# The first product of layer 2 by seven products of halves, weights streamed from DRAM

## The chip, the cores and the metric

The kernel runs on one core of a Trainium2 chip. Its time is the device time of one execution, in microseconds. The engines of the core have short names here: PE is TensorE's matmul (PEld its weight load), DVE VectorE, ACT ScalarE, POOL GpSimd, SP SyncE, which issues the DMAs.

## What is computed

Pooled attention, and behind it two feed-forward layers without residuals. All arrays are fp32; there are 4 batches, 8 heads, 576 positions of 64, hence 2304 tokens of 512, and both layers widen to 2048.

```python
def _attn_ref(q, k, v):
    k_p = k.reshape(B, H, Sp, pool, D).mean(axis=3)
    v_p = v.reshape(B, H, Sp, pool, D).mean(axis=3)
    scores = scale * np.matmul(q, k_p.transpose(0, 1, 3, 2))
    scores = scores - np.max(scores, axis=-1, keepdims=True)
    attn = np.exp(scores)
    attn = attn / (np.sum(attn, axis=-1, keepdims=True) + 1e-09)
    return np.matmul(attn, v_p)

def _moe_ref(x, w_in, w_out):          # layer 1
    h = x @ w_in
    g = np.where(h >= 1, h, np.where(h <= -1, 0.0, (h + 1) ** 2 / 4.0))
    return g @ w_out

def _moe2_ref(x, w_in, w_out):         # layer 2
    h = x @ w_in
    g = np.maximum(h, 0.0) + np.log1p(np.exp(-np.abs(h)))
    return g @ w_out
```

## The kernel before

The tokens are cut into five blocks of 512, 512, 512, 384 and 384 (BLK), the 2048 inner columns into 16 chunks of 128. Layer 1 runs block by block, chunk by chunk; layer 2 does the same after it. A chunk is one first product (emit_g1, matmul L387: four slices of the 512 inputs, out `h` in a PSUM bank), an activation (act) and one second product (emit_g2, matmul L452, summed over the 16 chunks in the PSUM banks `y`). The second product lags two chunks behind the first, so that PE has work while the activation runs.

But for the first block of layer 1, an fp32 operand is split into a high and a low part (whi and wlo of a weight, xh and xl of an input, gh and gl of an activation), and a product is three matmuls: high by high, high by low, low by high. In layer 2 the first product of a chunk is 12 matmuls of the block's 512 or 384 columns; the second takes 128 tokens at a time, three matmuls of 512 columns each. The activation of layer 2 (L411 to L432) is Abs, Exp and Ln on ACT, a subtraction on POOL (r), four operations on DVE and the split into gh and gl, on ACT and DVE.

Weights come as 64-bit floats. Those of layer 2 are converted during layer 1 in 32 units (convert2, L158; two words on ACT, exponents on DVE, a product on POOL, a sum and a split) that start at half step CONV2 = 48, three in ten half steps, and are stored to DRAM (`w2d`). In the last block of layer 1 w2_load (L182) brings them back, and they stay in SBUF during layer 2 as 32 tiles of the pool `w`. The output of layer 1 is split as it leaves PSUM (emit_y, L459: four ACT and four DVE operations a block), stored to `y1d`, and read back by x2_load (L364).

PE and SP follow the order of the code throughout. In layer 1 so do ACT, DVE and POOL (`order`), with the attention of the next block, the conversion units and the loads laid between the chunks by the tables PLAN, KV_PLAN and CONV2; in layer 2 a scheduler orders ACT, DVE and POOL.

Of the kernel before, what the change touches and what calls it, by code (L numbers as in the profile page):

```python
# [20 lines left out]
NP = H // 2  # L21
# [9 lines left out]
def pooled_attention_ffn_ffn(ctx, tc, q, k, v, v0, w1, w2, out):  # L31
# [26 lines left out]
    CONV2 = 48  # L58
    T0 = [sum(BLK[:j]) for j in range(NB)]
    TB = 128 * max(BLK)  # L60
# [11 lines left out]

    y1d = dram.tile([128, NB, 2, KD, TB], FP32, name="y1d")
    w2d = dram.tile([128, NC, 2, 2, DM], FP32, name="w2d")
# [17 lines left out]
    later = []  # L92

# [33 lines left out]
    def convert1(m):  # L127
# [10 lines left out]
        wt[0, *USE[m]] = af.rearrange("p (h f) -> p h f", h=2)  # L138
        yield

    def split1(m):

        hi, lo = (slot([128, 2, DM], FP32R, n) for n in ("whi", "wlo"))
        f = wt[0, *USE[m]]
# [3 lines left out]
        wt[0, *USE[m]] = (hi, lo)  # L148
        yield
# [7 lines left out]

    def convert2(n):  # L158
        a = es2.cv.tile([128, DM], U32, tag="a", bufs=3, name="a")
# [12 lines left out]
        b = es2.cv.tile([128, DM], U32, tag="b", name="b")  # L172
        hi, lo = b.bitcast(FP32R), a.bitcast(FP32R)
        nc.scalar.activation(out=hi, in_=af, func=ACTF.Copy)
        yield
        nc.vector.tensor_tensor(out=lo, in0=af, in1=hi.bitcast(FP32), op=ALU.subtract)
        yield
        for m, t in enumerate((hi, lo)):
            nc.sync.dma_start(out=w2d[:, n // 2, m, n % 2, :], in_=t.bitcast(FP32))
        yield  # L180

    def w2_load(m):  # L182
        wt[1, *USE[m]] = tuple(slot([128, 2, DM], FP32R, n) for n in ("whi", "wlo"))
        for n, t in enumerate(wt[1, *USE[m]]):
            nc.sync.dma_start(out=t.bitcast(FP32), in_=w2d[:, m, n])
# [63 lines left out]
    def kv_gen(b):  # L249
# [3 lines left out]
        if b > 1:  # L253
            for job in jobs[:3] if ring else jobs:
                kv_load(b, *job, ring)
            yield
        for m, job in enumerate(jobs):
# [3 lines left out]
            if ring and 0 < m < len(jobs) - 2:  # L261
# [10 lines left out]
    def tile_gen(i, j, wide=False):  # L272
# [85 lines left out]
    def x_tiles(f, j):  # L358
        xs[f, j] = (
# [4 lines left out]
    def x2_load(j):  # L364
        n = 128 * BLK[j]
        x_tiles(1, j)
        for m, x in enumerate(xs[1, j]):
            nc.sync.dma_start(out=x.bitcast(FP32)[:, :, 0:n], in_=y1d[:, j, m, :, 0:n])

    def whole(f, j):  # L370

        return (f, j) == (0, 0)

    def emit_g1(f, j, c):
        n = 128 * BLK[j]
        h = ps["h" if f == 0 or c % 2 else "h2"].tile([128, TB], FP32, tag="h", name="h")[:, 0:n]
        done = 0
        for kk in range(KD):
            cols = slice(kk * 128, (kk + 1) * 128)
            if whole(f, j):  # L380
                ops = ((wt[f, 0, c // 2][:, c % 2, cols], xs[f, j][0].bitcast(FP32)),)
            else:
                wh, wl = (t[:, c % 2, cols] for t in wt[f, 0, c // 2])
                xh, xl = xs[f, j]
# [319 lines left out]
```

## Time and profile before

| | us |
|---|---|
| three runs | 918.67, 918.76, 920.44 |
| median | 918.76 |
| the profiled execution | 918.5 |
| its span | 916.8 |
| PE / DVE / ACT / POOL busy | 892.3 / 541.1 / 486.6 / 137.1 |

The span is the time from the first to the last instruction of the profiled execution; the device time has 1.7 us around it. Busy times are sums over the whole span, while the kernel has stages with different limits (attention, layer 1 with the conversion beside it, layer 2), so the stretches of 20 us below tell more than the sums. In the timeline a matmul's duration overlaps the next one's, since matmuls are pipelined: what one costs is the distance of starts. A wait in the profile names the line that waits and the operation whose end released it.

### The profile page before, as it was taken

How to read it: one execution, taken by the hardware profiler on the slowest of the kernel's cores; microseconds unless marked ns; L12 is line 12 of the kernel's file. 1: busy time of each engine (PE TensorE's matmuls, PEld its weight loads, DVE VectorE, ACT ScalarE, POOL GpSimd, SP SyncE). 2: the span in 40 equal slices, each digit the busy share in tenths (PEclk: the TensorE clock that was granted, in tenths of full speed). 3: DMA queues.
4: the chain of work that ended last, by engine and by line, in shares of the span. 5: the costliest groups of instructions: out<-in, count | busy, mean ns of one | idle time of the engine just before them, and what ended most of it. 6: DMA issues, size and time to landing. Idle time of an engine off the chain costs nothing.

```text
span 916.8 us, 12048 instructions
## 1 busy us (share of the span) xinstructions
PE 892.3 (97%) x4442; PEld 715.2 (78%) x4442; DVE 541.1 (59%) x887; ACT 486.6 (53%) x931; POOL 137.1 (15%) x121
## 2 busy tenths in 40 slices
PE   8999999999999999899899899999999999999998
PEld 4444445788878888899899788888888888999896
DVE  6898773758678555767656434454445444544544
ACT  4766544566655545566655444444444443554544
POOL 0000000001111111111111112222222222222221
PEclk9999999999999999999999899999999999999999
DMA  7844510302465235424799910030003000300000
GB/s 255 331 149 163 207 44 37 125 12 69 143 224 185 85 111 195 146 97 140 258 397 395 341 54 0 1 138 1 1 0 115 1 1 1 116 0 1 35 1 35
DMA packets 37547, 105.64 MB, mean 115 GB/s; under 512 B 3888, under 2 KB 7984, under 8 KB 34672
## 3 DMA queue, kind: packets, MB, share of 16 engines
q1 hardware_dynamic: 37488, 104.87, 32.3%
q8 instruction: 35, 0.57, 0.3%
q14 instruction: 24, 0.20, 0.1%
HBM read 73.92 MB, written 30.93 MB: 114 GB/s over the span
## 4 chain that ended last, share of the span: by engine, by line
PE 83%; DVE 7%; ACT 4%; DMA 4%; issue 1%; POOL 0%; SPq 0%; DVEq 0%; ACTq 0%; POOLq 0%
PE y L452 39%; PE h L387 38%; DMA w2d<-b 2%; PE a L338 2%; PE a L324 2%; PE a L280 2%; DMA st<-in_w 2%; ACT e L313 1%; DVE gl L432 1%; DVE y L467 1%; DVE wf L108 1%; DMA kv<-in_k 1%; DVE ks L217 1%; PE vpa L243 1%; DVE wf L137 0%
## 5 line engine op out<-in xcount | busy, mean ns | idle before, releaser
L387 PE MATMUL h<-xh,whi 128*128 128x512 f32 (+1 forms) x576 | 213.4, 370 | 0.0
L387 PE MATMUL h<-xh,wlo 128*128 128x512 f32 (+1 forms) x576 | 210.7, 366 | 0.0
L387 PE MATMUL h<-xl,whi 128*128 128x512 f32 (+1 forms) x576 | 210.4, 365 | 0.0
L420 POOL TENSOR_TENSOR r<-e,r 128x512 f32<-128x512 f32 (+1 forms) x80 | 95.5, 1194 | 314.9 <-DVE r L417 296.9
L430 ACT ACTIVATE gh<-l 128x512 fp32r<-128x512 f32 (+1 forms) x80 | 47.1, 589 | 141.4 <-DVE l L425 137.8
L387 PEld LDWEIGHTS h<-xh,whi 128*128 128x128 f32 x576 | 108.3, 188 | 15.5 <-issue 1.6
L387 PEld LDWEIGHTS h<-xl,whi 128*128 128x128 f32 x576 | 108.3, 188 | 14.1 <-issue 0.5
L387 PEld LDWEIGHTS h<-xh,wlo 128*128 128x128 f32 x576 | 108.1, 188 | 12.7
L452 PE MATMUL y<-whi,gl 128*128 128x512 f32 x288 | 113.9, 395 | 1.5 <-DVE gl L432 1.5
L452 PE MATMUL y<-whi,gh 128*128 128x512 f32 x288 | 112.9, 392 | 2.0 <-ACT gh L430 2.0
L452 PE MATMUL y<-wlo,gh 128*128 128x512 f32 x288 | 113.5, 394 | 0.0
L165 POOL TENSOR_TENSOR l<-l,st 128x512 bf16<-128x512 bf16 x32 | 40.1, 1254 | 456.5 <-DVE st L112 390.6
L452 PE MATMUL y<-gl,whi 128*128 128x512 f32 (+1 forms) x256 | 93.9, 367 | 9.3 <-DVE gl L432 9.2
L398 ACT ACTIVATE t<-h 128x512 f32<-128x512 f32 (+1 forms) x80 | 44.5, 556 | 100.4 <-PE h L387 94.7
L452 PE MATMUL y<-gh,whi 128*128 128x512 f32 (+1 forms) x256 | 94.9, 371 | 0.0
L452 PE MATMUL y<-gh,wlo 128*128 128x512 f32 (+1 forms) x256 | 93.0, 363 | 0.0
L417 DVE TENSOR_SCALAR r<-e 128x512 f32<-128x512 f32 (+1 forms) x80 | 32.9, 412 | 95.0 <-ACT e L415 95.0
L432 DVE TENSOR_TENSOR gl<-l,gh 128x512 fp32r<-128x512 f32 (+1 forms) x80 | 52.1, 652 | 55.2 <-ACT gh L430 54.5
L414 ACT ACTIVATE e<-h 128x512 f32<-128x512 f32 (+1 forms) x80 | 44.5, 556 | 65.8 <-PE h L387 61.2
L404 DVE SCALAR_TENSOR_TENSOR t<-t,h 128x512 f32<-128x512 f32 (+1 forms) x64 | 39.5, 617 | 60.8 <-ACT t L399 60.6
L425 DVE TENSOR_TENSOR l<-l,r 128x512 f32<-128x512 f32 (+1 forms) x80 | 51.0, 638 | 36.7 <-POOL r L420 36.3
L452 PEld LDWEIGHTS y<-whi,gl 128*128 128x128 f32 x288 | 54.6, 189 | 13.8 <-DVE gl L432 2.4
(76 smaller groups left out, 1324.9 us busy)
## 6 DMA issues: line engine op xcount, KB each, us to landing
raw<-in_w SPq DMA_DIRECT2D x16, 1024.0 KB, 4.8
st<-in_w SPq DMA_DIRECT2D x32, 512.0 KB, 4.4
w2d<-b SPq DMA_DIRECT2D x32, 256.0 KB, 4.7
w2d<-a SPq DMA_DIRECT2D x32, 256.0 KB, 4.9
whi<-w2d SPq DMA_DIRECT2D x16, 512.0 KB, 8.6
wlo<-w2d SPq DMA_DIRECT2D x16, 512.0 KB, 8.8
y1d<-y SPq DMA_DIRECT2D x12, 512.0 KB, 3.8
kv<-in_k SPq DMA_DIRECT2D x16, 288.0 KB, 5.3
```

Source lines behind the costliest of these rows:

```text
L165: nc.gpsimd.tensor_tensor(out=l, in0=l, in1=e, op=ALU.mult)
L280: nc.tensor.matmul(out=pa[off:off + n, r * 512 + p * T:r * 512 + (p + 1) * T], lhsT=qt[rows, p, off:off + n], rhs=kps[b][rows, p, :], star ...
L387: nc.tensor.matmul(out=h, lhsT=a, rhs=b[:, kk, 0:n], start=(done == 0), stop=(done == len(ops) * KD - 1),)
L398: nc.scalar.activation(out=g, in_=h, func=ACTF.Relu, bias=1.0)
L404: nc.vector.scalar_tensor_tensor(out=g, in0=t, scalar=1.0, in1=h, op0=ALU.min, op1=ALU.max)
L414: nc.scalar.activation(out=e, in_=h, func=ACTF.Abs)
L417: nc.vector.tensor_scalar(out=r, in0=e, scalar1=1.0, scalar2=-1.0, op0=ALU.add, op1=ALU.add)
L420: nc.gpsimd.tensor_tensor(out=r, in0=e, in1=r, op=ALU.subtract)
L425: nc.vector.tensor_tensor(out=g, in0=g, in1=r, op=ALU.add)
L430: nc.scalar.activation(out=gh, in_=g, func=ACTF.Copy)
L432: nc.vector.tensor_tensor(out=gl, in0=g, in1=gh.bitcast(FP32), op=ALU.subtract)
L452: nc.tensor.matmul(out=o, lhsT=a, rhs=b, start=(c == 0 and n == 0), stop=(c == NC - 1 and n == len(ops) - 1),)
```

## The change

Layer 2 no longer goes by blocks. The tokens form three groups of 768 (NS), each two halves of 384 (SN), and the chunks are taken in pairs, eight pairs, so layer 2 has 24 steps (NQ). In a step the first product is a product of 2 x 2 blocks: token halves by halves of the 512 inputs, by halves of the pair's columns. It is computed with seven products (PRODUCTS, emit_product) in place of eight, by the scheme of Strassen and Winograd: x_gen builds the sums and differences of the input's blocks (four DVE operations, and seven splits on ACT and DVE) from the unsplit y1, convert2 those of the weights (t1 to t4). The seven products go to two PSUM banks in turn; ACT keeps three intermediate results (`s`) and copies the last, DVE adds three times (L828), and act2 does the activation on the two chunks, 128 x 768 each.

The second product (emit_group, six tiles of 128 tokens a half step) is laid between the seven products as filler: two tiles after each of the first five products, one after the last two; in a step the tiles of (step before last, half 1) come first, then those of (last step, half 0).

The weights no longer stay in SBUF: a step loads its own (wi_load, four DMAs, and wo_load, two, 2.88 MB together), two steps ahead for wi, so each weight is read three times. DRAM holds seven split blocks of weights for each pair (`wid`). x_gen for the first group runs in the last block of layer 1; for the others from the third step of the group before. emit_y now copies (two ACT, two DVE operations a block). CONV2 is 44. `ob` has the pool's two buffers instead of four, and `kv` and `q` of the attention have fewer buffers as well.

```diff
-    CONV2 = 48
+    CONV2 = 44
+    NS, SN = 3, 384
...
+            t = slot([128, 4, QK], FP32, "t")
+            t3, t2, t4, t1 = (t[:, m, :] for m in range(4))
+            nc.vector.tensor_tensor(out=t1, in0=b12, in1=b11, op=ALU.subtract)
+            nc.vector.tensor_tensor(out=t3, in0=b22, in1=b12, op=ALU.subtract)
+            yield
+            nc.vector.tensor_tensor(out=t2, in0=b22, in1=t1, op=ALU.subtract)
+            nc.vector.tensor_tensor(out=t4, in0=b21, in1=t2, op=ALU.subtract)
...
+    def wi_load(q, i):
+        n = min(2, NPR - 2 * i)
+        t = slot([128, n, 2, QK], FP32R, "wi")
+        nc.sync.dma_start(out=t.bitcast(FP32), in_=wid[:, q % NH, 2 * i:2 * i + n])
...
+        def hi(p, f):
+            if s == 1 and p < 4:
+                t = xpool.tile([128, 2, 2, SN], FP32R, tag=("xh", "xl")[p % 2], name="xf")
+                x2[s, p] = (t[:, 0], t[:, 1])
+            else:
+                x2[s, p] = tuple(slot([128, 2, SN], FP32R, n) for n in ("xfh", "xfl"))
+            nc.scalar.activation(out=x2[s, p][0], in_=f, func=ACTF.Copy)
+
+        def lo(p, f):
+            h, l = x2[s, p]
+            nc.vector.tensor_tensor(out=l, in0=f, in1=h.bitcast(FP32), op=ALU.subtract)
...
+        a22, a21 = load(1, 1), load(1, 0)
+        yield
+        a11, a12 = load(0, 0), load(0, 1)
+        yield
+        hi(3, a22)
+        yield
+        lo(3, a22)
+        s1 = a22
+        tt(s1, a21, a22, ALU.add)
...
+    for o in (8, 9, *range(12, 23)):
+        plan.setdefault(32 * LAST + o, []).append(("x", 0))
...
+    PRODUCTS = (0, 1, 0, 1, 0, 1, 0)
+    FRESH = (0, 1, 5)
+    def emit_product(q, p, o):
+        wh, wl = (wi[q, p][:, m, :] for m in range(2))
+        xh, xl = x2[q // NH, p]
+        done = 0
+        for kk in range(2):
+            cols = slice(kk * 128, (kk + 1) * 128)
+            for a, b in ((wh, xh), (wh, xl), (wl, xh)):
+                nc.tensor.matmul(
+                    out=o, lhsT=a[:, cols], rhs=b[:, kk, :],
+                    start=(p in FRESH and done == 0), stop=(done == 5),
...
-                ob = es2.t2.tile([128, DM], FP32, tag="ob", bufs=4, name="ob")
+            ob = es2.t2.tile([128, DM], FP32, tag="ob", name="ob")
...
+        for p, o in enumerate(banks[b] for b in PRODUCTS):
+            emit_product(q, p, o)
+            if p < 3:
+                keep[p] = gpool.tile([128, SN], FP32, tag=("t", "gh", "gl")[p], name="s")
+                nc.scalar.activation(out=keep[p], in_=o, func=ACTF.Copy)
+            elif p < 6:
+                h, x = ((ha[:, SN:], 2), (hb[:, SN:], 1), (ha[:, 0:SN], 0))[p - 3]
+                nc.vector.tensor_tensor(out=h, in0=o, in1=keep[x], op=ALU.add)
+            else:
+                nc.scalar.activation(out=hb[:, 0:SN], in_=o, func=ACTF.Copy)
+            if p == 5:
+                act2(q, 0, ha)
+            if p == 6:
+                act2(q, 1, hb)
+            if q == NQ - 1:
+                filler(1)
+            else:
+                filler(2 if p < 5 else 1)
...
+            if p == 2:
+                wo_load(q)
+            if q + 2 < NQ and p % 2 + (p == 6):
+                wi_load(q + 2, p // 2)
+            if xg and p in (1, 3, 5):
+                next(xg, None)
```

Three places show how instructions stand now. The first is ACT at the start of layer 2. Before, Abs (L414), Exp (L415) and Ln (L416) of the first two chunks stand between the four copies of layer 1's output (L466):

```order
L414 ACTIVATE e<-h 128x512 x2
L466 ACTIVATE y<-y_3726 128x384
L415 ACTIVATE e<-e 128x512
L466 ACTIVATE y<-y_3727 128x384
L415 ACTIVATE e<-e 128x512
L466 ACTIVATE y<-y_3728 128x384
L416 ACTIVATE l<-e 128x512
L466 ACTIVATE y<-y_3729 128x384
L416 ACTIVATE l<-e 128x512
```

On ACT in the changed kernel the same place, the first step (h_4508 is half 0, h_4509 half 1 of its result; L825 keeps an intermediate result, L830 copies the last product):

```order
L825 ACTIVATE s<-h 128x384 x3
L557 ACTIVATE y<-y_3859 128x384
L557 ACTIVATE y<-y_3861 128x384
L593 ACTIVATE e<-h_4508 128x768
L830 ACTIVATE h_4509<-h 128x384
L594 ACTIVATE e<-e 128x768
L593 ACTIVATE e<-h_4509 128x768
L825 ACTIVATE s<-h 128x384
L595 ACTIVATE l<-e 128x768
L594 ACTIVATE e<-e 128x768
L595 ACTIVATE l<-e 128x768
L602 ACTIVATE gh<-l 128x768 x2
```

Abs and Exp of half 1 and a copy of the next step now stand ahead of the Ln of half 0, and both gh come last.

The second place is PE in the first step of layer 2. Before, the first of the second product's matmuls (L452) follow twelve matmuls of a chunk's first product:

```order
L387 MATMUL h<-xh,whi 128x512
L387 MATMUL h<-xl,whi 128x512
L387 MATMUL h<-xh,wlo 128x512
L452 MATMUL y_4486<-whi,gh 128x512
L452 MATMUL y_4486<-wlo,gh 128x512
L452 MATMUL y_4486<-whi,gl 128x512
L452 MATMUL y_4487<-whi,gh 128x512
```

On PE in the changed kernel, the last matmuls of layer 1 (L543), and the first products (L582) that follow them without filler:

```order
L543 MATMUL y_3862<-gh,whi 128x384
L543 MATMUL y_3862<-gl,whi 128x384
L543 MATMUL y_3862<-gh,wlo 128x384
L582 MATMUL h<-xfh,wi 128x384
L582 MATMUL h<-xfl,wi 128x384
L582 MATMUL h<-xfh,wi 128x384 x2
L582 MATMUL h<-xfl,wi 128x384
L582 MATMUL h<-xfh,wi 128x384 x2
```

Twenty-four matmuls of L582 stand there in a row (the last three products of the first step, which have no filler, and the first product of the second), until the first tile of the second product comes, which needs gh of half 0:

```order
L582 MATMUL h<-xfl,wi 128x384
L582 MATMUL h<-xfh,wi 128x384
L619 MATMUL y_4645<-whi,gh 128x512
L619 MATMUL y_4645<-wlo,gh 128x512
L619 MATMUL y_4645<-whi,gl 128x512
L619 MATMUL y_4646<-whi,gh 128x512
L619 MATMUL y_4646<-wlo,gh 128x512
L619 MATMUL y_4646<-whi,gl 128x512
```

From there on six matmuls of 384 and mostly six of 512 alternate.

The third place is DVE in the last block of layer 1. Before, a chunk's two operations (L404, L432) stand beside one unit of the conversion:

```order
L404 SCALAR_TENSOR_TENSOR t<-t,h 128x384
L432 TENSOR_TENSOR gl<-t,gh 128x384
L170 TENSOR_TENSOR a<-a,l 128x512
L107 TENSOR_SCALAR st<-a 128x512
L108 SCALAR_TENSOR_TENSOR a<-a,st 128x512
L112 TENSOR_SCALAR st<-a 128x512
L404 SCALAR_TENSOR_TENSOR t<-t,h 128x384
L432 TENSOR_TENSOR gl<-t,gh 128x384
```

On DVE in the changed kernel (L264 and L267 are x_gen's, L220 the splits of weights, L118 to L184 a conversion unit):

```order
L517 SCALAR_TENSOR_TENSOR t<-t,h 128x384
L527 TENSOR_TENSOR gl<-t,gh 128x384
L220 TENSOR_TENSOR t<-t,b 128x512
L118 TENSOR_SCALAR st<-a 128x512
L119 SCALAR_TENSOR_TENSOR a<-a,st 128x512
L123 TENSOR_SCALAR st<-a 128x512
L264 TENSOR_TENSOR xfl<-x_3957,xfh 128x768
L220 TENSOR_TENSOR t<-t,b 128x512
L220 TENSOR_TENSOR a<-a,b 128x512
L264 TENSOR_TENSOR xfl<-x_3981,xfh 128x768
L267 TENSOR_TENSOR x_3955<-x_3955,x_3981 128x768
L517 SCALAR_TENSOR_TENSOR t<-t,h 128x384
```

Nine operations, three of a conversion unit, three splits of weights and three of x_gen, now stand between two chunks' activations there; before it was four.

## Rows read from the trace of the kernel before

**Rows 1.** The page: busy time, share of span and instructions of each engine

```profile
PE 892.3 (97%) x4442; PEld 715.2 (78%) x4442; DVE 541.1 (59%) x887; ACT 486.6 (53%) x931; POOL 137.1 (15%) x121
```

**Rows 2.** The page: the chain that ended last, shares by engine

```profile
PE 83%; DVE 7%; ACT 4%; DMA 4%; issue 1%; POOL 0%; SPq 0%; DVEq 0%; ACTq 0%; POOLq 0%
```

**Rows 3.** Stretches of 20 us: PE, PEld, DVE, ACT, POOL busy, clock, DMA share, GB/s

```profile
440.00:460.00 20.00, 17.26 (x100) 16.94 (x99) 14.95 (x27) 11.53 (x23) 3.81 (x3) 1.00 0.82 273
460.00:480.00 20.00, 18.15 (x105) 17.83 (x104) 10.60 (x19) 10.26 (x20) 2.65 (x2) 1.00 1.03 408
480.00:500.00 20.00, 19.49 (x112) 19.09 (x111) 15.02 (x25) 11.53 (x23) 3.82 (x3) 1.00 1.02 391
...
520.00:540.00 20.00, 17.14 (x64) 13.54 (x65) 9.99 (x16) 7.49 (x13) 4.17 (x3) 0.83 0.50 188
540.00:560.00 20.00, 20.00 (x90) 16.57 (x89) 9.03 (x15) 9.50 (x16) 3.88 (x3) 1.00 0.01 1
```

**Rows 4.** PE's waits, 505 to 917 us: total, times, longest

```profile
PE y L452 <- ACT gh L430: 2.0, 1, 2.0
PE y L452 <- DVE gl L432: 1.5, 1, 1.5
```

**Rows 5.** Timeline of PE, start of layer 2: start, duration, instruction

```profile
508.86 0.39 PE L387 MATMUL h<-xh,whi 128*128 128x512 f32 x1
...
511.62 0.39 PE L387 MATMUL h<-xh,whi 128*128 128x512 f32 x1
...
514.34 0.33 PE L452 MATMUL y<-gh,whi 128*128 128x384 f32 x1
...
518.98 0.39 PE L387 MATMUL h<-xh,wlo 128*128 128x512 f32 x1
...
528.58 0.40 PE L387 MATMUL h<-xl,whi 128*128 128x512 f32 x1
```

**Rows 6.** Timeline of all engines, the last instructions

```profile
912.51 0.40 PE L452 MATMUL y<-whi,gl 128*128 128x512 f32 x1
912.94 0.60 ACT L475 ACTIVATE ob<-y 128x512 f32<-128x512 f32 x1 [0.79 <-PE y L452]
```

**Rows 7.** Timeline of PE in the blocks of 384 tokens of layer 2

```profile
835.19 0.39 PE L452 MATMUL y<-whi,gh 128*128 128x512 f32 x1
...
837.27 0.33 PE L387 MATMUL h<-xh,whi 128*128 128x384 f32 x1
...
838.34 0.33 PE L387 MATMUL h<-xh,whi 128*128 128x384 f32 x1
...
839.38 0.39 PE L452 MATMUL y<-whi,gh 128*128 128x512 f32 x1
...
843.50 0.33 PE L387 MATMUL h<-xh,whi 128*128 128x384 f32 x1
```

**Rows 8.** Groups by line and form: busy us, mean ns, idle before; 1024 wide: 0-140 us

```profile
L415 ACT ACTIVATE e<-e 128x512 f32<-128x512 f32 x43 | 27.2, 632 | 1.3
L414 ACT ACTIVATE e<-h 128x384 f32<-128x384 f32 x31 | 15.3, 492 | 15.9 <-PE h L387 15.7
L145 ACT ACTIVATE whi<-wf 128x1024 fp32r<-128x1024 f32 x16 | 16.7, 1045 | 0.0
L421 DVE SCALAR_TENSOR_TENSOR l<-h,l 128x512 f32<-128x512 f32 x43 | 29.7, 691 | 9.8 <-ACT l L416 9.8
L421 DVE SCALAR_TENSOR_TENSOR l<-h,l 128x384 f32<-128x384 f32 x31 | 17.3, 558 | 5.7 <-ACT l L416 5.7
L108 DVE SCALAR_TENSOR_TENSOR wf<-wf,b 128x1024 uint32<-128x1024 uint32 x16 | 19.6, 1225 | 0.6
L420 POOL TENSOR_TENSOR r<-e,r 128x512 f32<-128x512 f32 x48 | 63.1, 1315 | 212.0 <-DVE r L417 194.0 <-PE y L452 18.0
```

**Rows 9.** DMA issues: times, KB each, median us to landing

```profile
out<-ob SPq DMA_DIRECT2D x18, 256.0 KB, 2.1
```

**Rows 10.** PE's waits, 140 to 509 us: total, times, longest

```profile
PE y L452 <- DVE gl L432: 9.2, 6, 2.7
```

More of the change, by code (lines that the diff above doesn't have):

```diff
@@ L92, in pooled_attention_ffn_ffn @@
     later = []
+    wi = {}
+    wo = {}
+    x2 = {}
     def slot(shape, dtype, name):
@@ L188, in batch_runs @@
+        yield
+        hi(6, s4)
+        yield
+        lo(6, s4)
+        yield
     def batch_runs(i):
@@ L362, in x_tiles, with whole, emit_g1 @@
         )
-    def x2_load(j):
+    def whole(j):
+        return j == 0
+    def emit_g1(j, c):
         n = 128 * BLK[j]
[L366 to L376, printed above, removed]
+        h = ps["h"].tile([128, TB], FP32, tag="h", name="h")[:, 0:n]
         done = 0
@@ L663, in pooled_attention_ffn_ffn @@
-    while pend:
-        emit_g2(*pend.pop(0))
+        if hot and c + 2 < NC:
+            next(c1[c + 2])
+        step(n - 1)
+        for g in splits:
+            next(g)
+        splits = []
+        step(n - 2)
+        if hot and c + 1 < NC:
+            next(c1[c + 1])
+        if hs == CONV2 - 4:
+            st_load(0)
+            st_load(1)
+        if hs >= CONV2:
+            tick(hs % 10 in (0, 3, 6))
+        background(hs)
+        while len(pend) > 2:
+            emit_g2(*pend.pop(0))
@@ new lines, in pooled_attention_ffn_ffn @@
+        step(n - 1)
+        next(acts[n])
+        if hot and c + 1 < NC:
+            next(c1[c + 1])
+        if hot and c + 4 < NC:
+            w_load(c + 4)
+        if hs + 1 >= CONV2:
+            tick((hs + 1) % 10 in (0, 3, 6))
+        background(hs + 1)
+        if j == 0 and c >= NC - 2 or j == 1 and c < NC - 2:
+            splits = [split1((c + 2) % NC)]
+            next(splits[0])
+        if j == LAST and c in (11, 12, 13, 14):
+            for i in range(2):
+                wi_load((c - 11) // 2, (c - 11) % 2 * 2 + i)
@@ new lines, in pooled_attention_ffn_ffn, with filler @@
+    while flight:
+        tick(False)
+    order.close()
+    esc.close()
+    es1.close()
+    es2.t2 = es2.enter_context(tc.tile_pool(name="t2", bufs=2))
+    ps["y2"] = es2.enter_context(tc.tile_pool(name="ps_y2", bufs=1, space=PSUM))
+    for m in (NB * NC - 2, NB * NC - 1):
+        for _ in acts.pop(m, ()):
+            pass
+    fill = [(emit_g2, (*s, (m,))) for s in pend for m in range(KD)]
+    NQ = NS * NH
+    xg = None
+    def filler(n):
+        for _ in range(min(n, len(fill))):
+            f, args = fill.pop(0)
+            f(*args)
@@ L665, in pooled_attention_ffn_ffn @@
+    for o, w in ((1, 1), (0, 0), (0, 1)):
+        fill += [(emit_group, (NQ - 1 - o, w, t)) for t in range(2 * SN // 128)]
+    filler(len(fill))
     es2.close()
```

371 lines of the change are left out of this document (204 added, 167 removed).

## The prediction, made before the changed kernel ran

> **What bounds the kernel now.** The page's busy shares come first: PE is at work for 892.3 of 916.8 us, the next engine, DVE, for 541 [rows 1]. The chain of work that ended last agrees: 83% of it is PE [rows 2]. Such shares are means, so the second view cuts the trace into stretches of 20 us. In layer 2 PE is busy all the time (20.00 of 20.00 at 540), ACT and DVE about half of it and DMA near nothing [rows 3]; the list of PE's waits from 505 us on holds only 2.0 and 1.5 us, both at the start of layer 2 [rows 4]. So layer 2 is priced by its matmuls. The end of layer 1 is different: from 440 to 500 PE loses 2.7, 1.9 and 0.5 us of each 20 while the DMA share is 0.82 to 1.03 and DVE is at 15 of 20 [rows 3].
>
> The profiled execution took 918.5 us for a span of 916.8; the median of the three runs is 918.76. I work in differences and add them to the 918.5, 0.3 under the median and well inside the 0.2% that I count as no change.
>
> **Part 1, the matmuls of layer 2.** First what they cost now. The first of layer 2 starts at 508.86, the last at 912.51 [rows 5, 6], with its own step of 0.23 that is 403.9 us. Not part of them are the 12 narrow matmuls that finish layer 1 (2.1 us) and the stall at the start: between the start at 518.98 and that at 528.58 lie 13 matmuls [rows 5], worth 13 x 0.229 = 3.0 of the 9.6 us, so about 6.4 is lost (waiting, and then matmuls at twice the usual spacing: the granted clock of 520 to 540 is 0.83, part of it at the lower of the two levels [rows 3]). There remain 395.4 us.
>
> The spacing of starts gives the price of one: in a chunk of two blocks that alternate, 12 matmuls of 384 columns take 837.27 to 839.38 = 2.11 us, the first six of them 1.07; 18 of 512 take 839.38 to 843.50 = 4.12, so 0.229 each [rows 7]; in an unbroken run of the wide ones 12 take 511.62 to 514.34 = 2.72, so 0.2267 [rows 5]. The new layer 2 has 24 steps of 7 products. A product is six matmuls of 384, between them stand 36 matmuls of 512 a step. At 1.07 for every six and 0.2315 for a 512 (nine of 512 between two stretches of 384, 835.19 to 837.27, run at that) a step is 7 x 1.07 + 36 x 0.2315 = 15.83 us, 24 steps 380.0. **That is -15.4 us**, although an eighth of the first product, 24 x 6 x 0.176 = 25 us, is gone: most of today's first product runs in 512 columns at 0.2267, which is 4.43 ns for ten columns, and 384 in 0.176 are 4.58; and the unbroken runs of 24 are cut into pieces of six, where each change of shape and back costs about 0.06, 7 times a step. The bounds: if the change of shape cost nothing, a step would be 42 x 0.1733 (the six from 838.34 to 839.38) + 36 x 0.2267 = 15.44, the sum 370.6, -24.8; if it cost twice as much, 390, -5.
>
> The Trainium skill, page "TensorE: Matmul & The Clock Gate", section "Back-to-back issue gap", gives an isolated matmul N/2.4 + 2.5 ns: 162.5 for 384 columns and 215.8 for 512. Worked out from it (an estimate), the saving would be 22.8. The rows show 173 to 178 and 227 to 231, so the trace does not agree, and its spacing decides; that page's time is near the one of rival (b).
>
> **Part 2, the other engines of layer 2.** A step adds three ACT copies and one to SBUF (384 wide, 0.49 each) and three DVE additions (0.56 each), and does the activation on tiles of 768. Durations of 768 lie between the rows of 512 and 1024 [rows 8]: ACT 0.63 and 1.05 give 0.84, DVE 0.69 and 1.23 give 0.96; POOL at 512 takes 1.32, so 1.97. ACT: 4 x 0.49 + 2 x 4 x 0.84 = 8.7 of 15.8 us; DVE: 3 x 0.56 + 2 x (3 x 0.96 + 0.6) = 8.6; POOL 3.9. None is near the bound. Latency matters more. From p5's last matmul to the first gh go a DVE addition, Abs, the copy of p6, Exp, Abs of the other half, a copy, Ln, two DVE operations on the half, the r of the other and gh: 0.43 + 0.56 + 0.84 + 0.49 + 0.84 + 0.84 + 0.49 + 0.84 + 0.96 + 0.6 + 0.96 + 0.84, with hand-overs about 9.2 us. In the steady state PE has five products and eight tiles (8 x 3 matmuls of 512) until it needs that gh: 5 x 1.07 + 24 x 0.2315 = 10.9. So the chain hides, with about 2 us to spare, gl a little less; the two PSUM banks come free 1.6 us or more before their next product. Weights: 2.88 MB a step in 15.8 us are 182 GB/s, under half of the 391 to 408 that the trace reaches [rows 3], and each load is issued 17 us or more of matmuls ahead of its use. I take zero for all of this. If the cover is gone, each step pays the difference, 24 x the shortfall.
>
> **The start of layer 2** has no such cover. Eight quarter chunks of layer 1 fill the first four products; then p4, p5, p6 and the p0 of the next step run bare, and the tiles of (step 0, half 0) wait for the chain above with only 2 x 1.07 + 0.23 us of work beside it: 9.2 - 2.4 = 6.8 us, gl 0.6 more. In the row a wait of 2 us and one of 1.5 drew matmuls at double spacing until 528.58, a loss of about 2.4 on top [rows 5]; I add 2.5. In the second step the additions queue on DVE behind those of x_gen for the next group (0.8), and in the third its half 0 is late again by about 1.5 and gl by 3.2, since x_gen's DVE operations wait for a load there and hold the queue, with 0.5 of clock loss. Sum 15.8, against 6.4 today: **+9.4**, bounds +3 (the later steps pay nothing and the first chain is 2 us shorter) and +13.
>
> **The tail.** Now the last matmul starts at 912.51, its copy ends at 913.54 and the span at 916.8, so 4.3 us [rows 6]. The last group has six tiles instead of three and ob has two buffers instead of four: a copy of the third and fifth tile waits until a store has landed, 2.1 us after its issue [rows 9]. Tile 1: copy to +1.1, landed about +3.5; tile 3: +4.1 and +6.5; tile 5: +7.1 and +9.5; tile 6 +10.5 on the other chain, counted from the start of tile 1's last matmul, while the last matmul starts at +3.45. So 7.3 instead of 4.3: **+3**. Bounds 0 (stores land at once) and +4.
>
> **Layer 1.** Gone: the weights' and inputs' loads in the last block, whose queue kept DMA at 0.89 to 1.03 [rows 3]. I give back 2.4 (what PE loses from 460 to 500) and 1.1 of the 2.7 of 440 to 460: -3.5. The bursts at a block's end are halved (no split of y1), -2 of the 9.2 us that PE waits there for gl [rows 10], a guess between 0 and -4. Added: for each of the eight pairs of chunks four DVE additions of 256 columns (some 0.42) and 1.1 us more of splits, 2.8 us, 22.6 in all, spread over blocks 1 to 4; and x_gen for group 0 in the last block, 11 DVE operations of 768 = 10.6 and 7 of ACT = 5.9. In the last block DVE then has per chunk of 4.15 us: 1.25 for the activation, 0.6 of a conversion unit at 3.6 = 2.2, and in five and a half chunks 10.6/5.5 = 1.9, so 5.35: an overload of 1.2 x 5.5 = 6.6 us, part of which falls into the slack of the two chunks that PE runs behind; I take +5 (0 to +10), and +1.5 for the other blocks. Net **+1**, from -5 to +10.
>
> **Sum.** -15.4 + 9.4 + 3 + 1 = -2.0, from the profiled execution's 918.5 to 916.5.
>
> **The rivals.** (a) Forecast, all terms near their middle: 912 to 921, around 916.5; chance 0.55, of it 0.36 below 916.9 and 0.19 within 0.2% of the median (that 0.2%, 1.8 us, is about what a measurement of this kernel can tell from no change). (b) Change of shape costs nothing: the term is -24.8 and the time 907. For it: the six matmuls right after a change took 1.07, only 0.025 above six others. Against: the 9 of 512 take 2.08 instead of 2.04. Chance 0.16. (c) VectorE becomes the bound in the last block: the 6.6 us of overload are not absorbed and each late gl (4 to 5 of them) draws a stretch at half the clock, 2.4 us each as at 520 [rows 5], so 6.6 + 4 x 2.4 = 16 instead of 5; 927. It decides the sign once layer 1 costs over +5 net. For it: DVE at 14.95 of 20 in 440 to 460 with PE waiting [rows 3], and gl being what PE waits for, six times [rows 10]. Chance 0.20. (d) The first product of a step waits for a bank copied out behind the long Exp: 0.75 x 23 = 17, 933. Against: the banks come free 1.6 us early. Chance 0.06. (e) The stream of weights is late and layer 2 is paced by DMA; at 182 of some 400 GB/s unlikely: 0.03, over 930.
>
> The range of 8 in 10 goes from 905 to 927: below it a tenth, of (b), above it (d), (e) and part of (c). Faster 0.36 + 0.16 = 0.52, same 0.20, slower 0.28.
>
> **What would show it.** Stretches of 20 us in layer 2 with PE at 20.00; 24 steps at 15.8 us (first matmul of one p0 to that of the next), 15.4 to 15.5 says (b), over 16 with waits on DVE or ACT in every step says the chain is not hidden or (d). PE's waits after the first L582: 6 to 8 us for gh at the first L619, then 1 to 5 in the next two steps; nothing there says the start was mis-sized. PE's busy time from 440 to the end of layer 1 with DVE at 19 or 20 of 20 says (c). From the last matmul to the span's end 7 to 8 us. The prediction is wrong if steps in the middle of layer 2 have a wait, or if layer 1 ends more than 8 us away from where it ends today.

## The result, and the profile after

The changed kernel takes 929.3 us in the median of four runs (926.3 to 930.4) against 919.0 for the kernel before: 1.0104 times as long, with an interval of 1.0078 to 1.013 (ratios here and below are of the means, 928.8 and 919.3 here, so they differ a little from those of the medians). It is slower by 10 us, where 2 us faster was forecast, and it lies 2 us above the upper end of the range (927).

The page of the changed kernel, where the first two lines answer to [rows 1] and [rows 2]; the others are groups of section 5 (busy us, mean ns, idle time before and what ended it):

```profile
PE 884.4 (95%) x4490; PEld 721.9 (78%) x4490; DVE 660.7 (71%) x903; ACT 511.6 (55%) x925; POOL 144.4 (16%) x89
...
PE 73%; DVE 14%; ACT 7%; DMA 3%; issue 2%; SPq 0%; DVEq 0%; ACTq 0%
...
L597 POOL TENSOR_TENSOR r<-e,r 128x768 f32<-128x768 f32 x48 | 102.9, 2143 | 310.3 <-DVE r L596 280.7
...
L598 DVE SCALAR_TENSOR_TENSOR l<-h,l 128x768 f32<-128x768 f32 x48 | 80.1, 1669 | 14.9 <-ACT l L595 14.9
...
L603 DVE TENSOR_TENSOR gl<-l,gh 128x768 fp32r<-128x768 f32 x48 | 77.2, 1607 | 8.8 <-ACT gh L602 8.7
```

PE has less to do, 884 us in place of 892, and yet the span grew from 916.8 to 928.3; DVE and ACT have taken 21% of the chain where they had 11% [rows 2]. The last two groups show where the forecast left the road: I had 0.96 us for such an operation of 768 columns, and they take 1.67 and 1.61.

Stretches of 20 us of the changed kernel, columns as in [rows 3]:

```profile
440.00:460.00 20.00, 17.18 (x83) 16.86 (x82) 13.19 (x25) 10.84 (x22) 2.64 (x2) 0.83 0.82 259
460.00:480.00 20.00, 19.68 (x114) 19.36 (x113) 16.25 (x29) 14.07 (x27) 3.65 (x3) 1.00 0.50 170
480.00:500.00 20.00, 16.90 (x89) 16.58 (x88) 18.76 (x29) 11.55 (x22) 3.95 (x3) 0.91 0.60 201
...
520.00:540.00 20.00, 12.46 (x52) 10.77 (x51) 11.32 (x13) 8.05 (x12) 4.27 (x2) 0.76 0.84 300
540.00:560.00 20.00, 16.86 (x83) 14.68 (x82) 11.71 (x13) 9.56 (x15) 4.27 (x2) 0.99 0.61 192
560.00:580.00 20.00, 17.67 (x76) 15.40 (x75) 11.91 (x13) 8.68 (x13) 4.29 (x2) 0.83 0.28 86
...
840.00:860.00 20.00, 20.00 (x102) 18.01 (x101) 11.72 (x14) 9.89 (x15) 4.29 (x2) 1.00 0.59 184
```

The waits of PE from 505 us on in the changed kernel (total, times, longest), to be set against [rows 4]:

```profile
PE y L619 <- DVE gl L603: 6.5, 6, 2.3
PE y L619 <- issue: 6.3, 1, 6.3
PE y L619 <- ACT gh L602: 3.1, 1, 3.1
PE h L582 <- DVE h L828: 0.4, 2, 0.3
```

The 6.3 us put down to "issue" is the first tile of the second product; in the timeline the gh that it needs ends at 532.29 and its matmul starts at 532.40.

The starts of the 24 steps (first matmul of one step to that of the next, in us, from the timeline of PE) say how much of this is where:

```
changed kernel           11.44 23.01 24.12 15.69 15.72 16.10 16.35 15.69 15.69 15.91 16.69 17.41 15.73 16.10 16.37 15.69 15.69 15.87 15.69 (four more of 15.69)
subtraction on DVE       11.44 21.40 20.71 15.69 (and 15.69 for the nineteen that follow)
five edits               10.92 19.79 17.06 16.95 15.69 (and 15.69, two of 15.68, for the eighteen that follow)
```

An undisturbed step is 15.69 us. The first has 8 pieces of layer 1 for filler and the second 6 tiles; the steps after them have 12. The account of the 11.5 us by which the span grew, each from the two timelines:

| | measured | forecast |
|---|---|---|
| matmuls of layer 2: 24 x 15.69 = 376.6 for 395.4 | -18.8 | -15.4 |
| losses in layer 2: 407.2 - 376.6 - 4.2 (24 narrow matmuls of layer 1) = 26.4 for 6.4 | +20.0 | +9.4 |
| of these up to 580 us / later | +13.5 / +6.5 | +9.4 / 0 |
| tail: 928.33 - 920.40 = 7.9 for 4.3 | +3.7 | +3 |
| layer 1, to the same point: 513.45 - 508.86 and 12 more matmuls left over (2.1) | +6.7 | +1 |

### The profile page after: what moved, and what is told of

The parts are those of the page before. It is cut to its first block, busy times and chain, and to the rows that moved or that the text cites. A ratio compares the mean times of both kernels' runs of the same rounds, so it can differ in the third digit from the quotient of the medians.

```text
span 928.3 us, 12445 instructions
## 1 busy us (share of the span) xinstructions
PE 884.4 (95%) x4490; PEld 721.9 (78%) x4490; DVE 660.7 (71%) x903; ACT 511.6 (55%) x925; POOL 144.4 (16%) x89
## 4 chain that ended last, share of the span: by engine, by line
PE 73%; DVE 14%; ACT 7%; DMA 3%; issue 2%; SPq 0%; DVEq 0%; ACTq 0%
PE y L543 18%; PE h L501 17%; PE y L619 17%; PE h L582 16%; DVE l L598 3%; PE a L400 2%; PE a L458 2%; DVE gl L603 1%; PE a L444 1%; DMA x<-y1d 1%; ACT e L433 1%; ACT e L593 1%; DVE wf L119 1%; DVE wlo L158 1%; ACT l L595 1%
## 5 line engine op out<-in xcount | busy, mean ns | idle before, releaser
L582 PE MATMUL h<-xfh,wi 128*128 128x384 f32 x544 | 161.7, 339 | 0.5 <-DVE h L828 0.4
L597 POOL TENSOR_TENSOR r<-e,r 128x768 f32<-128x768 f32 x48 | 102.9, 2143 | 310.3 <-DVE r L596 280.7
L582 PEld LDWEIGHTS h<-xfh,wi 128*128 128x128 f32 x544 | 101.9, 190 | 7.8 <-DVE h L828 2.4
L543 PE MATMUL y<-gl,whi 128*128 128x512 f32 (+1 forms) x256 | 95.0, 371 | 9.9 <-DVE gl L527 9.9
L501 PE MATMUL h<-xh,whi 128*128 128x512 f32 (+1 forms) x256 | 96.9, 378 | 0.0
L543 PE MATMUL y<-gh,whi 128*128 128x512 f32 (+1 forms) x256 | 95.6, 373 | 0.0
L501 PE MATMUL h<-xl,whi 128*128 128x512 f32 (+1 forms) x256 | 94.0, 367 | 0.0
L543 PE MATMUL y<-gh,wlo 128*128 128x512 f32 (+1 forms) x256 | 94.0, 367 | 0.0
L501 PE MATMUL h<-xh,wlo 128*128 128x512 f32 (+1 forms) x256 | 93.9, 367 | 0.0
L582 PE MATMUL h<-xfl,wi 128*128 128x384 f32 x272 | 92.7, 341 | 0.0
L598 DVE SCALAR_TENSOR_TENSOR l<-h,l 128x768 f32<-128x768 f32 x48 | 80.1, 1669 | 14.9 <-ACT l L595 14.9
L603 DVE TENSOR_TENSOR gl<-l,gh 128x768 fp32r<-128x768 f32 x48 | 77.2, 1607 | 8.8 <-ACT gh L602 8.7
L619 PEld LDWEIGHTS y<-whi,gl 128*128 128x128 f32 x288 | 54.8, 190 | 22.9 <-DVE gl L603 11.5
L619 PEld LDWEIGHTS y<-whi,gh 128*128 128x128 f32 x288 | 55.1, 191 | 15.6 <-issue 6.6
```

What stands on the lines that cost most here:

```text
L501: nc.tensor.matmul(out=h, lhsT=a, rhs=b[:, kk, 0:n], start=(done == 0), stop=(done == len(ops) * KD - 1),)
L543: nc.tensor.matmul(out=y[:, 0:128 * BLK[j]], lhsT=a, rhs=b, start=(c == 0 and n == 0), stop=(c == NC - 1 and n == len(ops) - 1),)
L582: nc.tensor.matmul(out=o, lhsT=a[:, cols], rhs=b[:, kk, :], start=(p in FRESH and done == 0), stop=(done == 5), skip_group_check=True,)
L597: nc.gpsimd.tensor_tensor(out=r, in0=e, in1=r, op=ALU.subtract)
L598: nc.vector.scalar_tensor_tensor(out=g, in0=h, scalar=0.0, in1=g, op0=ALU.max, op1=ALU.add)
L603: nc.vector.tensor_tensor(out=gl, in0=g, in1=gh.bitcast(FP32), op=ALU.subtract)
```

## The experiments

The theory from the account: the matmuls brought more than was forecast, and the loss lies in the activation chain (the operations on ACT, DVE and POOL between a first product and the matmuls that need its result), which DVE carries too slowly. In the changed kernel, DVE and POOL in a step with no wait of PE (timeline: start, duration, instruction, idle time before):

```profile
844.22 0.56 DVE L596 TENSOR_SCALAR r<-e 128x768 f32<-128x768 f32 x1 [1.85 <-ACT e L594]
845.33 2.26 DVE L598 SCALAR_TENSOR_TENSOR l<-h,l 128x768 f32<-128x768 f32 x1 [0.55 <-ACT l L595]
847.70 0.96 DVE L599 TENSOR_TENSOR l<-l,r 128x768 f32<-128x768 f32 x1
848.57 0.55 DVE L596 TENSOR_SCALAR r<-e 128x768 f32<-128x768 f32 x1
849.04 0.95 DVE L598 SCALAR_TENSOR_TENSOR l<-h,l 128x768 f32<-128x768 f32 x1
849.91 2.61 DVE L603 TENSOR_TENSOR gl<-l,gh 128x768 fp32r<-128x768 f32 x1
```

```profile
844.92 1.85 POOL L597 TENSOR_TENSOR r<-e,r 128x768 f32<-128x768 f32 x1 [8.91 <-DVE r L596]
849.27 2.44 POOL L597 TENSOR_TENSOR r<-e,r 128x768 f32<-128x768 f32 x1 [2.49 <-DVE r L596]
```

POOL works from 844.92 to 846.77; the DVE operation that starts inside, at 845.33, ends at 847.59, 0.82 behind POOL's end. The second POOL operation ends at 851.71; gl, started at 849.91, ends at 852.52, 0.81 behind it. The same operation on DVE, started at 849.04, ahead of POOL, takes its 0.95, and that POOL operation takes 2.44 instead of 1.85. So whichever is second runs when the first is done. The whole of layer 2 says the same: 27 of the 48 operations l<-h,l and 19 of the 48 gl start while POOL works, and each of these 46 ends 0.81 or 0.82 behind POOL's end; the other 50 take 0.94 to 0.96. In the kernel before the operation L421, at the same place of the chain, begins while POOL works and takes its usual 0.56; of its 80 in layer 2, 78 begin so and none takes longer for it:

```profile
841.27 0.56 DVE L421 SCALAR_TENSOR_TENSOR l<-h,l 128x384 f32<-128x384 f32 x1 [0.20 <-ACT l L416]
```

```profile
841.22 1.01 POOL L420 TENSOR_TENSOR r<-e,r 128x384 f32<-128x384 f32 x1 [3.17 <-DVE r L417]
```

There h is read from PSUM; the seven products leave h in an SBUF tile, and the operation has two tensors in SBUF.

**The subtraction on DVE.** It takes POOL out of layer 2.

```diff
-        nc.gpsimd.tensor_tensor(out=r, in0=e, in1=r, op=ALU.subtract)
+        nc.vector.tensor_tensor(out=r, in0=e, in1=r, op=ALU.subtract)
```

> The changed kernel with the subtraction of the activation of layer 2 (r) on DVE in place of POOL, so POOL is idle in layer 2. Theory (a DVE operation with two tensors in SBUF that starts while POOL works ends only behind POOL; in the new kernel the result h lies in SBUF and no more in PSUM, so one more operation is open to that): the operations l<-h,l and gl of 768 columns, 1.67 and 1.61 us in the mean now, fall to 0.95; DVE's busy time in layer 2 falls although it has 48 operations of 0.95 more; the waits of the second product's matmuls, 15.9 us in all now, fall by 4 to 7 us, the time by 5 us. Rival (DVE is simply slower at 768 columns on these operations): they stay at 1.6 us, DVE gets 48 x 0.95 = 46 us more to do, waits grow and the time rises by 2 us or more.

Measured: 916.3 us, 0.9975 of the kernel before (0.9956 to 0.9994), so 12 us faster than the changed kernel. Groups of DVE in layer 2 of this run (515 to 905 us):

```profile
L597 DVE TENSOR_TENSOR r<-e,r 128x768 f32<-128x768 f32 x48 | 45.8, 955 | 0.9
L598 DVE SCALAR_TENSOR_TENSOR l<-h,l 128x768 f32<-128x768 f32 x48 | 45.8, 953 | 0.3 <-ACT l L595 0.3
...
L603 DVE TENSOR_TENSOR gl<-l,gh 128x768 fp32r<-128x768 f32 x48 | 45.7, 951 | 4.9 <-ACT gh L602 4.6
```

Its waits of PE from 505 us on:

```profile
PE y L619 <- issue: 5.7, 1, 5.7
PE y L619 <- DVE gl L603: 2.8, 2, 2.3
PE y L619 <- ACT gh L602: 0.6, 1, 0.6
```

DVE does 45.8 us of work more and gets 66 back: the two groups fall from 80.1 and 77.2 to 45.8 and 45.7 us. All steps from the fourth on are 15.69; layer 2 takes 395.3 us (509.17 to the last matmul's start at 904.20, and 0.23) against 407.2. The rival, that DVE is simply slow at these operations, falls. The gain was twice the 5 us that I expected. In the list the waits fell from 16.3 to 9.1 us, while layer 2 fell by 11.9: a matmul that waits starts 0.2 to 0.4 us later still than its wait in the list says, counted from start to start, and waits under 0.15 are not in the list. The low clock took little part: behind the waits of the second and third step it cost 5.0 us instead of 6.0, and in the later steps of either run the granted clock is 1.00.

The edit changed more than the place of the subtraction. The scheduler, which orders ACT and DVE in layer 2, also laid other operations otherwise in steps 2, 3, 10 to 12 and 18. Of the 11.9 us, 3.7 were gained in stretches whose order is otherwise the same (steps 5 to 7, 13 to 15 and the end from step 24 on). In the others the order and POOL's hold are not separated, and a run below, with POOL still at the subtraction, takes 2.9 us off the third step by another order.

**The control: the same edit in the kernel before.**

> The kernel before, with the subtraction of the activation of layer 2 on DVE in place of POOL: a control for that edit. Theory (what POOL cost the changed kernel it did not cost here, since h is read from PSUM and PE has no wait in layer 2 but at its start): within 1.5 us of the kernel before, a gain of at most the 3.5 us of waits at the start and the clock behind them. Rival (the edit is good for 10 us wherever it stands): 8 us or more faster.

Measured: 916.8 us, 0.9986 (0.9974 to 0.9998): 1.3 us. So what POOL costs, it costs the changed kernel; the edit is hardly a gain in itself. What made it one, the operand in SBUF or the two halves that now stand close together, no run separates.

**One step later for x_gen.** DVE's x_gen operations also stand in the chain of the third step.

```diff
-        if m == 2 and s + 1 < NS:
+        if m == 3 and s + 1 < NS:
```

> The changed kernel with x_gen for the second and third group begun one step later (the fourth step of a group in place of the third). Theory (in the third step x_gen's operations stand on DVE ahead of the activation of the step before, and one of them waits for a load): the third step's waits for gh and gl, 3.1 and 2.3 us with the clock behind them, some 8 us in all from 540 to 580, fall below 3 us, the time by 4 us. Rival (DVE is short of time in these steps whoever is first, since operations wait for POOL): the waits stay above 4 us or come back a step later, the time within 2 us.

Measured: 925.7 us, 1.0078 (1.0063 to 1.0094), 2.4 us less than the changed kernel, between the two expectations. The third step falls from 24.12 to 18.67, but the fourth rises from 15.69 to 19.45: the waits come back a step later, so the rival was nearer. With POOL out of the way (the five edits, below) the two steps take 17.06 and 16.95.

**Pieces of layer 1 held back.** Four of the eight pieces that fill the first step move to where PE waits: behind its last two products and the first of the second step.

```diff
-                filler(2 if p < 5 else 1)
+                filler((2, 2, 0, 0, 0, 2, 1)[p] if q == 0 else 2 if p < 5 else 1)
```

> The changed kernel with the last four of the eight pieces of layer 1's second product moved behind the last two products of the first step and the first of the second, where PE now waits 6.5 us for gh and 1.6 for gl. Theory (the wait is the length of the activation chain less the work beside it): the four pieces are 2.1 us, so the first wait falls from 6.5 to 4.4 us, the time by 2 us. Rival (the chain itself is held by these pieces, since the copies of layer 1's output then come into it on ACT and DVE): the chain grows by 2 x 0.49 us on ACT and 2 x 0.56 on DVE, the wait falls by 1 us or less and the time stays within 1 us.

Measured: 926.1 us, 1.0077 (1.0053 to 1.01); the first wait falls from 6.3 to 4.0 us and the second step from 23.01 to 20.08. The theory holds: the wait is the chain less what lies beside it, here 2.3 us less for the 2.1 us of the four pieces.

**The tail.**

```diff
-            ob = es2.t2.tile([128, DM], FP32, tag="ob", name="ob")
+            ob = slot([128, DM], FP32, "ob") if s == NS - 1 else es2.t2.tile([128, DM], FP32, tag="ob", name="ob")
```

> The changed kernel, with the six output tiles of the last group each in a tile of the large weight pool of their own, so that no copy at the end waits for a store. Theory (two ob buffers make the tail): from the last matmul's start to the end of the span 7.9 us now, 4.3 to 5 us then, the time 3 us lower. Rival (the tail is the time of the stores themselves, six where there were three): 7 us or more stays, the time unchanged. Nothing else moves by more than 1 us in either case.

The end of the changed kernel (timeline; the copies wait for a store):

```profile
920.40 0.39 PE L619 MATMUL y<-whi,gl 128*128 128x512 f32 x1
920.78 4.98 SPq L635 DMA_DIRECT2D out<-ob  x5
921.84 0.69 DVE L625 COPY ob<-y 128x512 f32<-128x512 f32 x1 [3.04 <-DMA out<-ob]
922.93 0.60 ACT L627 ACTIVATE ob<-y 128x512 f32<-128x512 f32 x1 [2.17 <-DMA out<-ob]
924.71 0.69 DVE L625 COPY ob<-y 128x512 f32<-128x512 f32 x1 [2.18 <-DMA out<-ob]
```

With six tiles, the last copy starts at 921.90, 0.42 behind the last matmul's start at 921.48, and the span ends at 926.94: a tail of 5.5 instead of 7.9. The gain is 2.5 us in the trace (926.8 us, 1.008, 1.0049 to 1.0111). 1.2 us of the tail's growth are not the buffers'; that they are the stores of six tiles is likely, but no run tells.

**Layer 1 without x_gen's DVE operations.** In `lo` and `tt` of x_gen, for the first group, nothing is done and xfl is xfh, so the numbers computed are others; loads, ACT's copies and all matmuls stay.

```diff
+            if s == 0:
+                return
```

> The changed kernel without DVE's part of x_gen for the first group, in the last block of layer 1: the sums and differences and the low parts are left out (the high part stands in for the low one), so 11 DVE operations of 0.95 us are gone there; loads, ACT's copies and all matmuls stay. Theory (DVE is overloaded in the last block): PE's losses from 440 us to the start of layer 2, 11.4 us now, fall by 4 to 6 us (the wait of 3.1 us for gl at 481 and the clock behind it go), the time by 5 us. Rival (the stalls there come of the conversion units and their stores): losses and time unchanged within 1 us.

Measured: 919.0 us, 1.0004 (0.9984 to 1.0024). Its stretches where the changed kernel has 17.18, 19.68 and 16.90:

```profile
440.00:460.00 20.00, 17.18 (x91) 16.86 (x90) 14.33 (x27) 10.83 (x23) 3.81 (x3) 0.91 0.85 277
460.00:480.00 20.00, 20.00 (x117) 20.00 (x116) 15.59 (x29) 16.01 (x31) 2.66 (x2) 1.00 0.59 198
480.00:500.00 20.00, 20.00 (x117) 20.00 (x117) 11.16 (x19) 11.56 (x23) 2.34 (x2) 1.00 0.83 286
```

The wait at 481 us is gone, that at 445 is not. Layer 2 starts at 505.3 here; in the seven executions whose layer 1 is that of the changed kernel it starts at 508.9 to 513.7, 511.4 in the mean. So x_gen's 10.5 us on DVE cost about 6 us in the last block (by one execution, against seven that differ by up to 5 among themselves), and the theory of an overloaded DVE holds: from 480 to 500 DVE has 11.16 us to do for 18.76. The whole time is 9 us lower; the rest lies in layer 2 (403.0 us for 407.2). The scheduler ordered ACT and DVE otherwise in steps 3 to 7 there, which gained 1.7 us; in the other steps, of the same order, the waits are nearly those of the changed kernel and the time behind them is shorter.

**The conversion's product on DVE.**

```diff
-        nc.gpsimd.tensor_tensor(out=l, in0=l, in1=e, op=ALU.mult)
+        nc.vector.tensor_tensor(out=l, in0=l, in1=e, op=ALU.mult)
```

> The changed kernel with the product of the weights' conversion (bf16, 512 columns, 1.25 us on POOL, 32 times in layer 1) on DVE. Theory (in layer 1 too a DVE operation with two tensors in SBUF waits for POOL): DVE gets 32 x 0.4 = 13 us more to do, but its stretched operations (gl of 384 columns 0.69 in the mean against 0.55) come back, so its busy time from 200 to 500 us rises by less than 5 us, PE's waits for gl in layer 1, 9.9 us, fall by 2 us or more, the time by 2 us or more. Rival (DVE's own load in the last block decides): waits for gl rise by 2 us or more, the time too.

Measured: 921.0 us, 1.0032 (1.0016 to 1.0047). The low part of the 384-wide activation in layer 1 (200 to 510 us), first in the changed kernel, then here:

```profile
L527 DVE TENSOR_TENSOR gl<-t,gh 128x384 fp32r<-128x384 f32 x30 | 19.8, 661 | 0.0
```

```profile
L527 DVE TENSOR_TENSOR gl<-t,gh 128x384 fp32r<-128x384 f32 x32 | 17.7, 552 | 1.5 <-ACT gh L525 1.5
```

DVE takes over 31 products of 0.43, 13 us, and is busy for only 4.3 us more in 200 to 500 (227.6 for 223.2); PE's waits for gl fall from 9.9 to 8.2 us, a little less than the 2 expected. The same hold by POOL is at work in layer 1. The time fell by more than that (7 us), and more than half of it in layer 2 (402.5 us for 407.2), where the third step is 21.2 for 24.1. Nothing in the edit reaches there but the scheduler, and it did order otherwise. On ACT in the third step, the Exp of half 1 stands ahead of the Ln of half 0 in the changed kernel, and here behind it:

```profile
550.89 0.84 ACT L594 ACTIVATE e<-e 128x768 f32<-128x768 f32 x1
551.63 0.84 ACT L595 ACTIVATE l<-e 128x768 f32<-128x768 f32 x1
```

```profile
545.45 0.84 ACT L595 ACTIVATE l<-e 128x768 f32<-128x768 f32 x1
546.18 0.84 ACT L594 ACTIVATE e<-e 128x768 f32<-128x768 f32 x1
```

DVE's order moves with it (l of half 0 now stands ahead of r of half 1), and PE's waits in this step fall from 5.5 to 3.5 us. So an edit anywhere can move some us in layer 2 by the order alone.

**An eighth product.** What is the seventh-for-eighth saving worth?

```diff
             emit_product(q, p, o)
+            if p == 4:
+                emit_product(q, p, o)
```

> The changed kernel with the fifth product of every step done twice, so 48 matmuls of 384 a step in place of 42 (the result is then another; no other engine has more to do). It measures what the seventh-for-eighth saving is worth here. If PE is the bound of the steps (forecast): 24 x 6 x 0.175 = 25 us more, less about 1 us in the first two steps where the extra product lies beside a wait: +23 to +26. If another engine or the stream of weights paced the steps: clearly less, +15 or under.

Measured: 949.6 us, 1.0338 (1.0317 to 1.0358), 21.5 us more than the changed kernel and a little under the range; layer 2 grows from 407.2 to 428.5. An undisturbed step takes 16.73 for 15.69, so 1.04, 25 over 24 steps, and the rest is taken back in the steps with waits. PE is the bound of the undisturbed steps; POOL, ACT, DVE and the stream of weights are not.

**The changed kernel again, and the versions that follow.** Beside it the five edits together (subtraction, conversion's product, tail, pieces held back, x_gen a step later), those with x_gen at its old place and the conversion begun earlier, and the kernel before with both moves from POOL to DVE.

> The changed kernel as it is, on the same chip as the next three, so that they can be set against it. Between 1.006 and 1.012 of the kernel before. Theory on its spread (the waits are the same in each execution, but how long the clock stays low behind one is not): PE's waits are within 1 us of those of the first trace, the losses by the clock are not.

> The changed kernel with five edits together: subtraction of layer 2's activation on DVE, product of the conversion on DVE, output tiles of the last group each in a tile of its own, four pieces of layer 1 held back for the first wait, x_gen one step later. If the gains add (0.0129 + 0.0072 + 0.0024 + 0.0027 + 0.0026 of the kernel before, from 1.0104): 0.983 of the kernel before, some 903 us. If they overlap (the wait that one edit shortens is the one that another hides, and DVE gets fuller by both moves from POOL): 0.990, some 909 us.

> As the five edits together, but x_gen where the changed kernel has it, and the conversion begun four half steps earlier (CONV2 = 40). Theory (DVE is overloaded in the last block by conversion and x_gen together): conversion then ends two chunks earlier in the last block, the losses from 440 us to the start of layer 2 fall by 1 to 2 us more; the steps of layer 2 with x_gen cost 2 us more than in the five edits: same time as those within 2 us. Rival (x_gen's place no longer matters once POOL is out of the way): 1 to 2 us faster than the five edits.

> The kernel before with both moves from POOL to DVE (activation of layer 2 and conversion), the like of what the five edits contain: which of the two ways to compute the product is ahead when neither is slowed by POOL. Expected: the move in layer 2 gave 0.9986 of the kernel before, the one in layer 1 has fewer waits to take here (9.2 us for gl, of which 2 to 3 go): 0.994 to 0.998, some 914 us, so 5 to 10 us behind the five edits.

| | us | of the kernel before | interval |
|---|---|---|---|
| changed kernel | 927.1 | 1.0103 | 1.0085 to 1.012 |
| five edits | 906.0 | 0.9872 | 0.9857 to 0.9887 |
| x_gen early, CONV2 = 40 | 916.3 | 0.9981 | 0.9961 to 1.0002 |
| kernel before, two moves | 913.1 | 0.9945 | 0.9926 to 0.9964 |

In the changed kernel run again PE's waits from 505 us on are 16.8 us, for 16.3 in the first trace.

The gains do not quite add (0.983 was the sum), but the five edits beat both kernels, by 12 us and 21 us, and the kernel before with the two moves by 7 us; this last is the nearest that the runs have to a like-for-like comparison of the two ways to compute the product. PE's waits from 505 us on are, in the five edits,

```profile
PE y L619 <- ACT gh L602: 4.1, 2, 3.5
PE y L619 <- DVE gl L603: 2.5, 3, 1.3
```

The version with x_gen early was a miss for both theories: the last block took 72.6 us instead of 75.6, as expected, but the blocks before it 6 us longer already by the end of block 1 (257.9 for 252.0), where the earlier conversion meets the splits of layer 1's weights (argued from the order, no run shows it); and the third step is 22.2 again, 5 us. Both edits were changed at once, so how far the second comes of x_gen's place alone is not separated; the five edits against it suggest it.

## Why the prediction was wrong

**The matmuls** were right in kind and 3.4 us too dear: a step is 15.69 and not 15.83. Of the bounds, 15.44 to 16.2, the trace lies nearer to the first; a change of shape and back costs 0.036 us, not 0.06 (15.69 - 15.44 = 0.25, by 7).

**"I take zero for all of this"** in part 2 is the step that failed. The durations of 768 columns were interpolated between rows of DVE [rows 8], and every one of these rows was an operation alone, or one that reads PSUM: L421, the row of the sum, runs beside POOL in the kernel before and is not held, since h stood in PSUM. I carried its time over to an operation whose h stands in SBUF: 0.96 us each for l and gl, where they took 1.67 and 1.61 in the mean. The later steps of layer 2 lost 6.5 us where I had none, and the forecast's own sign of being wrong was there, waits in the middle of layer 2 (0.4, 0.4, 1.2 and 0.4 us in steps 7, 11, 12 and 15). With the subtraction on DVE layer 2 takes 395.3; my sum for it was 380.0 + 4.2 + 15.8 = 400.

The Trainium skill says this, on the page "SBUF — State Buffer", section "SBUF: two separate sides": the port pair that DVE and GpSimd share is "an exclusive lock, not a bandwidth split"; a DVE operation with two SBUF inputs and a GpSimd operation that reads SBUF exclude each other for the whole instruction. The trace agrees: the 46 operations l and gl that start while POOL works end 0.81 or 0.82 us behind its end, where they take 0.95 alone. And the trace of the kernel before had the sign: gl, with both inputs in SBUF, in layer 1 beside POOL's conversion (150 to 505 us), and in layer 2, where POOL is done by then (540 to 905):

```profile
L432 DVE TENSOR_TENSOR gl<-t,gh 128x384 fp32r<-128x384 f32 x31 | 21.4, 692 | 0.0
```

```profile
L432 DVE TENSOR_TENSOR gl<-l,gh 128x384 fp32r<-128x384 f32 x30 | 16.8, 558 | 18.2 <-ACT gh L430 17.6 <-PE h L387 0.7
```

I had not asked which operands the change moves to SBUF, nor what it brings side by side: gl had both inputs in SBUF before as well, and in layer 2 one of 80 was held there (1.75 us, at the start), while in the changed kernel the subtraction of one half falls on the gl of the other 19 times in 48.

**The start of layer 2** was mis-sized by 4 us, and not in its waits: 12.9 forecast, 13.0 in the list. That they agree is luck in part: the first wait was right (6.8 forecast, 6.3 measured, the chain of gh 9.2 and 8.6 us from p5's last matmul), but with the subtraction on DVE only 9.1 of the 13.0 are left, so part of the waits that I forecast came of a hold that was not in the forecast. What the low clock behind the waits costs was set at 3, and took about 6 of the 20 us lost up to 580; the granted clock is 0.76 from 520 to 540 and 0.83 from 560 to 580, and from 535 to 540 it is 0.50, the lower of its two levels. (In the row for the kernel before, 14 distances of 0.229 and not 13 give the 6.4 us that the prediction used; 13 would give 6.6.)

**Layer 1** was +1 and came out at +6.7 in the profiled execution, +4.6 in the mean of seven. x_gen's 6 us is near the +5 that I took. What failed is the credit: -3.5 for the loads that are gone and -2 for the bursts. From 460 to 480 PE did get back 1.5 us (19.68 for 18.15). The wait at 445 us is as long as before (17.18 of 20 for 17.26), with the DMA share again at 0.82, now by the stores of converted weights and the loads of x_gen and of the conversion; and the new wait at 481 took what was left.

**The tail** was +3 and is +3.7: 2.5 of it by the mechanism named, as the run with six tiles shows, and 1.2 that were not in the sum.

**The rivals.** None of them is what happened; (b) falls, since a step is 15.69 and not 15.44. (c) named the right engine and nearly the right end, 927, but by a price in the last block of layer 1 that was not paid; (d) and (e) fall, since the undisturbed steps have no wait. Missing among the rivals was a DVE that is slower than its rows because of another engine.

## What to carry to other kernels

Before a duration is carried over to a new operation, ask where its operands stand and what runs beside it: a DVE operation that moves from one PSUM and one SBUF input to two SBUF inputs can begin to wait for POOL, and the row of the old one will not show it (here 0.56 us at 384 columns for h in PSUM, 0.95 or up to 2.61 at 768 for h in SBUF). A saving in the bounding engine is safe only where the chain beside it has room, and this room is found by adding the chain with held durations; here 19 us were saved in matmuls and more than all given back. A stage that starts a pipeline anew is priced by its chain and by the clock that falls behind each wait, so one long activation (768 wide) in place of several short ones cost 6.3 us of wait at the start here, where the kernel before had 2.0. And where a scheduler orders the engines, an edit changes the order too: compare the orders before a gain is put down to the edit.

## What the runs showed of the hardware

The waits of PE repeat from execution to execution, what the clock does behind them does not. The stretch 440 to 460 us of the changed kernel has 17.18 us of work above, with the clock granted at 0.83; two runs with the same layer 1, first with the pieces of layer 1 held back, then with six output tiles:

```profile
440.00:460.00 20.00, 17.18 (x99) 16.86 (x98) 14.70 (x27) 10.86 (x22) 3.81 (x3) 1.00 0.85 278
```

```profile
440.00:460.00 20.00, 17.18 (x92) 16.87 (x91) 14.10 (x26) 12.11 (x25) 3.09 (x3) 0.91 0.78 246
```

The same wait is followed by 99, 92 or 83 matmuls in the same stretch, so a wait of 3 us costs between 3 and 6. That is why layer 2 begins anywhere between 508.9 and 513.7 us with the same instructions before it, and it may be why one kernel with such waits repeats less well (913.4 to 919.5 in ten runs with the subtraction on DVE) than one with fewer (905.4 to 907.1 in four runs of the five edits); the runs are too few to show that.
